# Three weight loads and the copies of shifted rows moved from SyncE's DMA queue to ScalarE's and GpSimd's

## The chip, the core and the metric

The kernel runs on one core of a Trainium2 chip. A core has five engines with an instruction stream each: TensorE (PE in the profile; its weight loads are PEld), VectorE (DVE), ScalarE (ACT), GpSimd (POOL) and SyncE (SP), which computes nothing and issues DMAs here. ACT and POOL can issue DMAs too. An engine works through its stream in order, and a wait for a semaphore holds back everything behind it in the same stream. The transfers themselves run on 16 DMA engines that all queues share.

The metric is the device time of one execution in microseconds (us); lower is better.

## What is computed

Two branches over one layer-normalised input, added to it. S = 2048 tokens, D = 448, 16 heads of 28, F = 1792, all inputs bf16.

```python
xn = layernorm(x)
# A: linear attention with learned feature maps
q, k, v = split_heads(xn @ wqkv)
phi = lambda t: concat(softmax(t @ w_phi), softmax(-(t @ w_phi)))
kv, z = phi(k)^T v, sum over tokens of phi(k)          # per head
attn = (phi(q) kv / (phi(q) z + 1e-6)) @ wo
# B: token shift and MLP, on xn again
h  = gelu(layernorm(xn) @ w1)
hs = concat(h[:, 0:112] one token later, h[:, 112:224] one earlier,
            h[:, 224:336] two later, h[:, 336:448] two earlier) @ w2
x1 = xn + hs
mlp = x1 + gelu(layernorm(x1) @ w3) @ w4
out = x + attn + mlp
```

## The kernel before

Everything stays in SBUF. Tokens are cut into 16 tiles of 128 (index `i`), features into chunks of up to 128. The kernel is first recorded: each call of `R.mm`, `R.act`, `R.ew`, `R.dma` and `R.dma_t` notes an instruction with the bytes it writes and reads, and `Recorder.solve` (L76) then derives the semaphore waits. So all instructions of a kind share a line in the profile (matmul L204, PE transpose L208, activation L212, elementwise on DVE or POOL L216, DMA transpose L219, DMA copy L222), and tiles are told apart by their names. The order of the calls is the order on each engine; it is written by hand, in three parts.

**The start (L366 to L388).** Loads are issued at once from SP and ACT: `xtok` (the tokens, in nine pieces), `wv`, `w1`, each weight in two halves, one per queue. SP goes on with the later tokens, `wphi`, and DMA transposes of `wqkv` columns into `wT`.

**The first phase, `chain([...])` (L949 to L969).** It normalises the tokens (`ln_stats` on DVE, `ln_scale` on POOL, `ln1_apply` on DVE or POOL; `ln1_sums(1)`, L470, gets the sums of tile 1 on ACT), transposes them into `xnT`, and runs the products with `wv` (`ZV`), with `w1` (`ZW` for the first 384 columns of h, `ZR` for the rest), and the folding of `w_phi` into the query and key weights (`FO`, whose result DVE casts into `wpq` and `wpk`). Pairs of matmuls on 64 rows each run on the two halves of the array; `chain` decides how the two halves interleave. Of its entries these matter here:

- `h_shift(gg)` (L669): h, transposed, lies in `hT` from column `OFF`; six DMA copies from SBUF to SBUF put rows 64 to 127 of each chunk, shifted by one or two tokens, into the front columns of `hT`. `gg` is the half of the tokens. `h_shift(0)` belongs to the entry `ZR(0, ...)` and is recorded when `chain` takes the last matmul of that entry's upper half; by then the next entry, `("p", 14)`, has been recorded, so POOL normalises tile 14 first. `h_shift(1)` stands near the end of the list.
- `rest_T(h)` (L666): a DMA transpose of the last 64 columns of h into `hRT`, on SP.
- `late_3` (L432): POOL clears the padding of `phik`, all of `kvq`, and part of `eq`. `kv_ones` (L438) then writes four blocks of ones into `kvq` on DVE.
- `kv_picks` (L731): POOL clears `pick`, DVE copies four blocks into it.
- `load_w2`, `load_w4` (L390, L395) and `load_lap(w3, B_w3)` (L358): weight loads, on SP, at the places where they stand in the list. `load_lap` takes the queues as its third argument.

**The second phase, `play([...])` (L1034 to L1054).** Here PE alternates between key and query products (`k0`, `k1`, `q0`, `q1`), the products of shifted h with `w2` (`w0`, `w1_`), kv tiles (`K`), the MLP with `w3` (`a`, `b`), attention numerators (`N`) and the final sums (`f`). Around the keys: ACT takes exponentials into `phik` (`k_exp`), DVE sums them (`kn`, L710), POOL multiplies by the reciprocal (`kx`, `k_product`, L717; eight products of two tiles each), and `K` i reads the result of `kx` i // 2. `sc`, `A` and `G` are the second layer norm: POOL's scale, the normalisation on POOL or DVE (`on_dve` lists tiles 4, 6, 7, 9, 12) into `g_tok`, and SP's DMA transpose into `gT`. The last `kx` is recorded as reading `g_tok`, so it waits for the normalisations of tiles 4 to 7. `wo_in` (L1030) loads `wo` between `kx` 5 and `kx` 6 of the list (counted from 0; the products 6 and 7 counted from 1).

Of the kernel before, what the change touches and what calls it, by code (L numbers as in the profile page):

```python
# [6 lines left out]
ACT = mybir.ActivationFunctionType  # L7
# [217 lines left out]
def bass_parallel_sum__linear_kernel_hedgehog__mixer_s_mlp__prompt_kernel(  # L225
    nc, A_x, A_wqkv, A_w_phi, A_wo, B_x, B_w1, B_w2, B_w3, B_w4, out,
):
    _, S, D = A_x.shape
# [6 lines left out]
    NH, REST = 3, 384  # L235
# [7 lines left out]
    with es:  # L243
        R = Recorder(nc, es)
# [9 lines left out]
        def view(h, cols, dt=BF16, at=0):  # L254
            a = h[:, at // 2:at // 2 + cols * DTB[dt] // 2]
            return a if dt == BF16 else a.bitcast(dt)

        def new(name, cols, dt=BF16):
            return view(region(name, cols * DTB[dt]), cols, dt)
# [13 lines left out]
        hT = view(hT_r, NH * HW).rearrange("p (m s) -> p m s", m=NH)  # L273
# [19 lines left out]
        w2 = new("w2", KC * D).rearrange("p (m d) -> p m d", m=KC)  # L293
        wo = wv
        w3 = new("w3", KC * F).rearrange("p (c f) -> p c f", c=KC)
        w4 = new("w4", FC * D).rearrange("p (c d) -> p c d", c=FC)
# [51 lines left out]
        dve, pool = "DVE", "POOL"  # L348


        def load_x(i, n, eng="SP"):
            R.dma(xtok[:, i:i + n, :], x2d[128 * i:128 * (i + n), :].rearrange("(j p) d -> p j d", p=128), eng)
# [5 lines left out]
        def load_lap(dst, src, engs=("SP", "SP")):  # L358
            for h in range(2):
                R.dma(dst[:, 2 * h:2 * h + 2, :], src[192 * h:192 * h + 256, :].rearrange("(c p) d -> p c d", p=128), engs[h])  # L360

        def load_half(dst, src, h, eng="SP"):
            R.dma(dst[:, 2 * h:2 * h + 2, :], src[192 * h:192 * h + 256, :].rearrange("(c p) d -> p c d", p=128), eng)
# [10 lines left out]
        load_x(5, 1, "ACT")  # L374
        load_half(w1, B_w1, 1)
        load_half(w1, B_w1, 0, "ACT")
        load_x(6, 2)
        load_x(8, 4)
        load_x(12, 4)
# [7 lines left out]
        load_wT(1, (0, 1, 2, 3))  # L387
        load_wT(0, (0,))  # L388

        def load_w2():  # L390
            R.dma(w2[:, 0:NH, :], B_w2[0:REST, :].rearrange("(m p) d -> p m d", p=128))
            for h in range(2):
                R.dma(w2[64 * h:64 * h + 64, NH, :], B_w2[REST:D, :])

        def load_w4():  # L395
            R.dma(w4[:, :, :], B_w4.rearrange("(c p) d -> p c d", p=128))

        vp = vaug.rearrange("p t (h e) -> p (t h) e", e=VP)

# [95 lines left out]
        def fold(t, m, b, n):  # L495
            def side(k, hi):
                r, c0, c1 = (slice(64, CR), 2 * DH, CR) if hi else (slice(0, 64), 0, 3 * DH)
                return [(banks[b + k][:, CR * c + c0:CR * c + c1],
                         wT[r, t, c, START[m + k]:START[m + k] + 128], bd[r, CR * c + c0:CR * c + c1], n == 0 and c == 0)
                        for c in range(NC)]  # L500
            return side(n, 0), side(1 - n, 1)
# [7 lines left out]
        def xn_T(i, b, n=1):  # L509
            return tuple([(xn_t(b)[:, h, 256 * j + 64 * kc:256 * j + 64 * kc + 64],  # L510
                           xn[lo:hi, i + j, 128 * kc:128 * kc + 128], ident[lo:hi, lo:hi], None)
                          for j in range(n) for kc in range(KC)] for h, (lo, hi) in enumerate((LO, HI)))
# [113 lines left out]
        def z_v(i, b):  # L626
            o = banks[b][:, 0:D]

            def make(rows, kcs):
                lo, hi = rows  # L630
                return [(o, xnT[lo:hi, kc, 128 * i:128 * i + 128], wv[lo:hi, kc, :], rows == LO and n == 0)
                        for n, kc in enumerate(kcs)]
            return make
# [11 lines left out]
        def z_w1(g, m, b):  # L645
            def make(rows, kcs):
                lo, hi = rows
                return [(banks[b], w1[lo:hi, kc, 128 * m:128 * m + 128], xnT[lo:hi, kc, 512 * g:512 * g + 512],
                         rows == LO and n == 0) for n, kc in enumerate(kcs)]
            return make  # L650
# [18 lines left out]
        def h_shift(gg):  # L669
            for m, r0, r1, q in ((0, 64, 112, 0), (1, 64, 96, 1), (2, 64, 80, 2), (0, 112, 128, 1), (1, 96, 128, 2),  # L670
                                 (2, 80, 128, 3)):
                s0 = max(0, 1024 * gg + SHIFTS[q])
                s1 = min(S, 1024 * gg + 1024 + SHIFTS[q])
                c0 = OFF + s0 - SHIFTS[q]
                R.dma(hT[r0:r1, m, s0:s1], hT[r0:r1, m, c0:c0 + s1 - s0])

        def w2_pair(i, b, heavy=None):
            def side(k, hi, rest):
# [223 lines left out]
        def do(f, *args):  # L902
            return "do", lambda: f(*args), ()

        def L(*ops):
            return do(ln1, *ops)

        def FO(t, m, n):
            return "both", fold(t, m, fb[t, m], n), ((fold_out, t, m, fb[t, m]),) if n else ()

        def XT(i, b, n=1, eng="ACT"):
            return "both", xn_T(i, b, n), ((xn_out, i, b, n, eng),)
# [4 lines left out]
        def ZV(i, *then):  # L917
            return "zip", z_v(i, vb[i]), then

        def ZW(g, m, *then):  # L920
            return "zip", z_w1(g, m, gb[g][m]), then

        def inside(n, job, inner):
            return (*job, (n, inner))

        def ZR(h, b, *then):
            return "zip", z_rest(h, b), then

        def EV(i, eng="ACT", n=1):
            return v_out, i, vb[i], eng, n  # L930

        def EW(g, m, n):
            return w1_out, g, m, gb[g][m], n
# [6 lines left out]
        def HF(p, n):  # L940
# [19 lines left out]
            ZW(1, 2, EW(1, 2, 1)), L(("p", 12), ("r", 15, 1)), inside(3, ZV(8, EV(8, "ACT", 1)), FO(1, 0, 0)), L(("m", 14)),  # L960
            XD(11), L(("r", 14, 1)), do(load_wT, 0, (1, 2, 3)), L(("a", 13)), inside(1, ZV(10, EV(10, "ACT", 1)), FO(1, 0, 1)),
            L(("a", 15)), ZR(0, 7, (rest_out, 0, 7), (rest_T, 0), (h_shift, 0)), ZV(9, EV(9, "DVE", 1)), XT(12, 3, 1, "ACT"),
            L(("p", 14)), do(load_w2), XT(13, 1, 1, "ACT"), ZV(11, EV(11, "ACT", 1)), ZW(2, 2, EW(2, 2, 1)), do(late_3),
            XT(14, 2, 2, "DVE"), ZW(2, 0, EW(2, 0, 1)), ZW(2, 1, EW(2, 1, 1)), do(load_lap, w3, B_w3), FO(1, 2, 0),
            inside(3, ZW(3, 0, EW(3, 0, 1)), FO(1, 2, 1)), ZR(1, 6, (rest_out, 1, 6)),
            inside(3, ZW(3, 2, EW(3, 2, 1)), FO(0, 0, 0)), ZV(15, EV(15, "ACT", 1)), do(kv_ones),
            inside(3, ZW(3, 1, EW(3, 1, 1)), FO(0, 0, 1)), do(rest_T, 1), inside(1, ZV(14, EV(14, "ACT", 1)), FO(0, 2, 0)),
            FO(0, 2, 1), ZV(13, EV(13, "ACT", 1)), ZV(12, EV(12, "DVE", 1)), HF(0, 0), do(kv_picks), HF(1, 0), HF(2, 0), HF(0, 1),
            do(h_shift, 1), HF(1, 1), do(load_w4), HF(2, 1)], 600, 1)  # L969

        on_dve = (4, 6, 7, 9, 12)
# [51 lines left out]
        def f(n, k):  # L1023
            fp[k][n - 1]()
# [3 lines left out]
            o_T(i)  # L1028

        def wo_in():  # L1030
            load_lap(wo, A_wo)

        K, G, S, T, kc, kb = kv_tile, g_T, store, q_T, kv_copy, kv_blocks
        play([  # L1034
# [4 lines left out]
            (w0, 8), (k1, 5), (q0, 5), (kx, 4), (K, 5), (lo, 4), (w1_, 8), (kn, 5), (q1, 5), (K, 6), (k0, 6), (w0, 10),  # L1039
            (k1, 6), (kx, 5), (q0, 6), (w1_, 10), (lo, 5), (q1, 6), (k0, 7), (K, 7), (kn, 6), (k1, 7), (q0, 7), (lo, 6),  # L1040
            (K, 8), (q1, 7), (lo, 7), (w0, 12), (kn, 7), (wo_in,), (kx, 6), (a, 0), (sc, 4), (w1_, 12), (b, 0), (A, 4),
            (G, 4), (A, 6), (K, 9), (A, 5), (G, 5), (G, 6), (a, 1), (K, 10), (A, 7), (K, 11), (b, 1), (a, 2), (K, 12),
            (b, 2), (kx, 7), (a, 3), (w0, 14), (a, 4), (G, 7), (lo, 9), (b, 3), (K, 13), (b, 4), (K, 14), (K, 15), (a, 5),
# [45 lines left out]
```

## Time and profile before

| What | Value |
|---|---|
| Time, median of 3 runs | 174.12 us (174.02 to 174.18) |
| The profiled execution | 174.06 us, span 172.3 us |
| PE busy / DVE / ACT / POOL | 97% / 64% / 48% / 52% of the span |
| DMA issues on SP / ACT / POOL | all but six / six / none |
| SP's issue of `w2` (3 DMAs), from 24.39 us | 2.56 us |
| SP's issue of `h_shift(0)`, from 28.31 us | 4.55 us |
| SP's issue of `w3` (2), from 32.90 us | 1.14 us |
| SP's issue of `h_shift(1)`, from 35.41 us | 3.85 us |
| SP's issue of `w4` (1), from 39.30 us | 0.59 us |
| SP's issue of `wo` (2), from 64.57 us | 1.09 us |

The span is the time from the first to the last instruction of the program in the profiled execution; the time of a run has 1.76 us around it. A timeline row gives its start and length in us, the engine, the line, the operation, what it writes and reads (`out<-in`) with shapes, how many instructions are merged (x3), and in brackets how long the engine sat idle before it and who ended that wait. SPq and ACTq are the parts of those engines that issue DMAs. Names have their numbers removed, so `w` stands for `w1`, `w2`, `w3` and `w4`, `vaug` also for buffers that later share its space. PE's busy time is modelled and its instructions overlap, so 97% doesn't mean that it is at its peak, but it does mean that there is next to no gap in which PE could catch up.

The chain of waits starts at the last instruction and goes back, at each step to what released the instruction or to the one before it on its engine. What is on it set the end.

### The profile page before, as it was taken

How to read it: one execution, taken by the hardware profiler on the slowest of the kernel's cores; microseconds unless marked ns; L12 is line 12 of the kernel's file. 1: busy time of each engine (PE TensorE's matmuls, PEld its weight loads, DVE VectorE, ACT ScalarE, POOL GpSimd, SP SyncE). 2: the span in 40 equal slices, each digit the busy share in tenths (PEclk: the TensorE clock that was granted, in tenths of full speed). 3: DMA queues.
4: the chain of work that ended last, by engine and by line, in shares of the span. 5: the costliest groups of instructions: out<-in, count | busy, mean ns of one | idle time of the engine just before them, and what ended most of it. 6: DMA issues, size and time to landing. Idle time of an engine off the chain costs nothing.

```text
span 172.3 us, 5315 instructions
## 1 busy us (share of the span) xinstructions
PE 166.9 (97%) x2308; PEld 96.6 (56%) x2308; DVE 110.9 (64%) x251; ACT 82.0 (48%) x107; POOL 90.0 (52%) x121
## 2 busy tenths in 40 slices
PE   7799999999999999999999999999999999999994
PEld 7545888874555555554544554554545545555563
DVE  3799943749999989918955873525817416474621
ACT  4478876777987899646133322133133212044000
POOL 5456970004779999860574289332441522724540
PEclk9999999999999999999999999999999999999999
DMA  5995546499998955161057557554961120233331
GB/s 127 330 248 92 104 67 158 87 352 220 334 159 174 135 124 138 21 76 30 11 114 97 111 105 146 94 103 106 136 135 34 30 57 4 57 34 84 88 87 50
DMA packets 51111, 20.07 MB, mean 116 GB/s; under 512 B 42256, under 2 KB 50384, under 8 KB 51088
## 3 DMA queue, kind: packets, MB, share of 16 engines
q1 hardware_dynamic: 49968, 18.86, 56.0%
q10 hardware_dynamic: 1120, 0.87, 1.6%
q8 instruction: 18, 0.29, 0.8%
q14 instruction: 5, 0.04, 0.1%
HBM read 7.14 MB, written 1.84 MB: 52 GB/s over the span
## 4 chain that ended last, share of the span: by engine, by line
PE 92%; DMA 3%; ACT 1%; DVE 1%; issue 0%; ACTq 0%
PE banks L204 91%; DMA wv<-in_A_wqkv_dram 3%; PE banks L208 1%; ACT xnT L212 1%; DVE wpq L216 1%; ACT vaug L212 0%; ACTq L222 0%; ACT L366 0%; DVE vaug L216 0%
## 5 line engine op out<-in xcount | busy, mean ns | idle before, releaser
L212 ACT ACTIVATE phik<-banks 128x1024 bf16<-128x1024 f32 (+1 forms) x44 | 42.2, 986 | 63.6 <-PE banks L204 63.4
L204 PE MATMUL banks<-gT,w 64*128 64x512 bf16 x392 | 49.2, 376 | 0.1
L216 DVE TENSOR_TENSOR vaug<-banks,vaug 128x464 f32<-128x464 f32 (+3 forms) x65 | 32.8, 513 | 20.6 <-PE banks L204 18.9
L204 PE MATMUL banks<-w,phik 64*128 64x448 bf16 (+3 forms) x434 | 45.2, 343 | 0.0
L216 POOL TENSOR_TENSOR xnT<-vaug 128x196 bf16<-128x196 f32 (+1 forms) x32 | 18.1, 587 | 47.8 <-DVE vaug L216 47.8
L204 PE MATMUL banks<-wv,xnT 64*128 64x448 bf16 (+3 forms) x222 | 32.8, 346 | 1.4 <-DMA wv<-in_A_wqkv_dram 1.2
L204 PEld LDWEIGHTS banks<-w,phik 64*128 64x128 bf16 (+1 forms) x434 | 22.9, 94 | 19.4 <-issue 0.4
L722 POOL TENSOR_TENSOR phik<-phik,rks 128x1792 bf16<-128x1792 bf16 x8 | 25.6, 3214 | 10.7 <-DVE rks L216 10.5
L204 PEld LDWEIGHTS banks<-gT,w 64*128 64x128 bf16 x392 | 18.0, 94 | 18.7 <-PE banks L204 1.1
L204 PEld LDWEIGHTS banks<-wv,xnT 64*128 64x128 bf16 (+1 forms) x222 | 13.8, 94 | 10.0 <-ACT xnT L212 1.6
L216 POOL TENSOR_TENSOR vaug<-xn,xtok 128x448 f32<-128x448 bf16 x16 | 16.2, 1033 | 0.2 <-DVE vaug L216 0.2
L216 DVE TENSOR_REDUCE ksum<-phik 128x64 f32<-128x1792 bf16 x8 | 16.0, 1994 | 0.0
L216 POOL TENSOR_TENSOR rs<-mv,mhalf 128x1 f32<-128x1 f32 (+2 forms) x18 | 12.4, 694 | 6.6 <-DVE mv L216 6.6
L204 PE MATMUL banks<-xnT,w 64*128 64x512 bf16 x84 | 15.7, 377 | 0.0
L216 DVE RECIPROCAL vaug<-banks 128x16 f32<-128x16 f32 x16 | 4.0, 252 | 17.4 <-PE banks L204 17.4
L204 PE MATMUL banks<-wpk,xnT 64*128 64x448 bf16 x112 | 14.9, 350 | 0.1
L212 ACT ACTIVATE hi<-banks 128x896 bf16<-128x896 f32 x16 | 13.8, 931 | 1.0 <-PE banks L204 1.0
L204 PE MATMUL banks<-wpq,xnT 64*128 64x448 bf16 x112 | 14.2, 349 | 0.0
L204 PE MATMUL banks<-w,hT 64*128 64x448 bf16 x96 | 12.9, 349 | 0.0
L216 DVE TENSOR_TENSOR xn<-banks,xn 128x512 bf16<-128x512 f32 (+1 forms) x16 | 9.0, 606 | 3.0 <-PE banks L204 2.9
L216 DVE BATCH_NORM_STATS2 st<-xn 128x6 f32<-128x448 bf16 x16 | 9.4, 589 | 0.0
L216 DVE BATCH_NORM_STATS2 st<-xtok 128x6 f32<-128x448 bf16 x15 | 9.1, 606 | 0.0
(72 smaller groups left out, 165.4 us busy)
## 6 DMA issues: line engine op xcount, KB each, us to landing
w<-in_B_w_dram SPq DMA_DIRECT2D x2, 896.0 KB, 5.7
out_dram<-vaug SPq DMA_DIRECT2D x15, 112.0 KB, 2.0
w<-in_B_w_dram SPq DMA_DIRECT2D x1, 1568.0 KB, 10.0
xtok<-in_A_x_dram SPq DMA_DIRECT2D x2, 448.0 KB, 7.4
wv<-in_A_wo_dram SPq DMA_DIRECT2D x2, 224.0 KB, 2.9
xtok<-in_A_x_dram SPq DMA_DIRECT2D x3, 112.0 KB, 2.6
xtok<-in_A_x_dram ACTq DMA_DIRECT2D x3, 112.0 KB, 2.8
w<-in_B_w_dram SPq DMA_DIRECT2D x1, 336.0 KB, 4.3
```

The costliest lines, as they stand in the source:

```text
L204: self.op("PE", lambda e: e.matmul(out, lhsT, rhs, start=start, stop=stop, skip_group_check=True), [out], [lhsT, rhs], tile=self._tile(lhsT))
L208: self.op("PE", lambda e: e.transpose(out, in_, ident), [out], [in_, ident], tile=self._tile(in_))
L212: self.op("ACT", lambda e: e.activation(out, in_, func, **kw), [out], [in_] + aps)
L216: self.op(eng, lambda e: getattr(e, name)(out, *args, **kw), [out], aps)
L722: R.op(pool, lambda e: e.tensor_tensor(ph, ph, wide, op=ALU.mult), [ph], [ph, wide, *after])
```

## The change

`w2` is issued by ACT right behind the ACT half of `w1`, at the very start, instead of by SP after the entry `("p", 14)`. The twelve copies of `h_shift` and the loads of `w3`, `w4` and `wo` keep their places in the order of calls, but POOL issues them instead of SP. ACT gets three more issues, POOL seventeen (six, two, six, one, two), SP loses twenty. What is transferred and computed stays the same; the waits that the copies need (for ACT's gelu, and of the second six for the first) go with them to POOL.

```diff
         load_half(w1, B_w1, 0, "ACT")
+        def load_w2():
+            R.dma(w2[:, 0:NH, :], B_w2[0:REST, :].rearrange("(m p) d -> p m d", p=128), "ACT")
+            for h in range(2):
+                R.dma(w2[64 * h:64 * h + 64, NH, :], B_w2[REST:D, :], "ACT")
+
+        load_w2()
         load_x(6, 2)
...
-        def load_w2():
-            R.dma(w2[:, 0:NH, :], B_w2[0:REST, :].rearrange("(m p) d -> p m d", p=128))
-            for h in range(2):
-                R.dma(w2[64 * h:64 * h + 64, NH, :], B_w2[REST:D, :])
-
         def load_w4():
-            R.dma(w4[:, :, :], B_w4.rearrange("(c p) d -> p c d", p=128))
+            R.dma(w4[:, :, :], B_w4.rearrange("(c p) d -> p c d", p=128), pool)
...
-                R.dma(hT[r0:r1, m, s0:s1], hT[r0:r1, m, c0:c0 + s1 - s0])
+                R.dma(hT[r0:r1, m, s0:s1], hT[r0:r1, m, c0:c0 + s1 - s0], pool)
...
-            L(("p", 14)), do(load_w2), XT(13, 1, 1, "ACT"), ZV(11, EV(11, "ACT", 1)), ZW(2, 2, EW(2, 2, 1)), do(late_3),
-            XT(14, 2, 2, "DVE"), ZW(2, 0, EW(2, 0, 1)), ZW(2, 1, EW(2, 1, 1)), do(load_lap, w3, B_w3), FO(1, 2, 0),
+            L(("p", 14)), XT(13, 1, 1, "ACT"), ZV(11, EV(11, "ACT", 1)), ZW(2, 2, EW(2, 2, 1)), do(late_3),
+            XT(14, 2, 2, "DVE"), ZW(2, 0, EW(2, 0, 1)), ZW(2, 1, EW(2, 1, 1)), do(load_lap, w3, B_w3, (pool, pool)), FO(1, 2, 0),
...
         def wo_in():
-            load_lap(wo, A_wo)
+            load_lap(wo, A_wo, (pool, pool))
```

On POOL the new issues stand in this order among its own work: the normalisation of tile 14, the six copies of `h_shift(0)`, the memsets of `late_3`, `w3`, the memset of `pick`, the six copies of `h_shift(1)`, `w4`, then the products of `kx` 0 to 5 (with the second layer norm of tiles 0 to 3 among them), `wo`, `kx` 6, the second layer norm of tiles 4 to 7, `kx` 7.

## The prediction

> **What bounds the kernel now.** I read the engine shares first, then the chain of waits in order of time, then the timelines of the engines whose queues the change touches.
>
> ```profile
> PE 166.9 (97%) x2308; PEld 96.6 (56%) x2308; DVE 110.9 (64%) x251; ACT 82.0 (48%) x107; POOL 90.0 (52%) x121
> PE banks L204 91%; DMA wv<-in_A_wqkv_dram 3%; PE banks L208 1%; ACT xnT L212 1%; DVE wpq L216 1%; ACT vaug L212 0%; ACTq L222 0%; ACT L366 0%; DVE vaug L216 0%
> ...
> 1.74 5.70 DMA wv<-in_A_wqkv_dram
> ...
> 30.18 1.10 DVE wpq L216
> ...
> 86.56 83.30 PE banks L204 x1012
> ```
>
> PE sets the end. The only transfer on the chain is the load of `wv`, which both kernels issue at the same place; after 31.3 us the chain is PE alone, but for four gaps of 0.05 us and the last 0.36 us. So nobody that matters waits for SP's queue, and emptying that queue earns nothing by itself. What can happen is that PE is made to wait. POOL is at 52% over the span, but a share of a span is an average; its timeline tells where it is full:
>
> ```profile
> 21.13 0.77 POOL L216 TENSOR_SCALAR xn<-xtok,rs 128x512 bf16<-128x512 bf16 x1
> 21.96 1.86 POOL L434 MEMSET phik<- 128x2048 bf16 x1
> 23.77 0.52 POOL L216 MEMSET kvq<- 128x512 bf16 x1
> ...
> 41.10 3.21 POOL L722 TENSOR_TENSOR phik<-phik,rks 128x1792 bf16<-128x1792 bf16 x1 [8.44 <-DVE rks L216]
> ...
> 60.37 9.55 POOL L722 TENSOR_TENSOR phik<-phik,rks 128x1792 bf16<-128x1792 bf16 x3
> 69.89 1.02 POOL L216 TENSOR_TENSOR rs<-mv,mhalf 128x4 f32<-128x4 f32 x1
> 71.00 0.20 POOL L216 TENSOR_SCALAR rs<-mv 128x4 f32<-128x4 f32 x1
> 71.42 1.03 POOL L216 TENSOR_SCALAR g_tok<-xn,rs 128x512 bf16<-128x512 bf16 x1 [0.22 <-POOL rs L216]
> 72.68 3.21 POOL L722 TENSOR_TENSOR phik<-phik,rks 128x1792 bf16<-128x1792 bf16 x1 [0.23 <-DVE g_tok L216]
> ```
>
> From 60.37 to 75.9 POOL works almost without a pause on the normalised keys, and PE follows it closely (PE's timeline):
>
> ```profile
> 75.31 0.39 PE L204 MATMUL banks<-vaug,phik 64*128 64x59 bf16 x16
> 75.55 0.81 PE L204 MATMUL banks<-gT,w 64*128 64x512 bf16 x6
> 76.19 0.62 PE L204 MATMUL banks<-vaug,phik 64*128 64x59 bf16 x32
> ```
>
> The last pair of kv tiles (76.19) reads the product that POOL ends at 72.68 + 3.21 = 75.89: 0.30 us of slack. At the start the engines that feed PE are as tight (timelines of ACT and DVE):
>
> ```profile
> 3.51 0.58 ACT L474 ACTIVATE xn<-xtok 128x448 bf16<-128x448 bf16 x1 [1.43 <-DMA xtok<-in_A_x_dram]
> ...
> 5.94 0.26 DVE L216 BATCH_NORM_AGGREGATE mv<-st 128x2 f32<-128x9 f32 x2
> 7.03 1.06 DVE L216 TENSOR_SCALAR xn<-xtok,mv,rs 128x512 bf16<-128x512 bf16 x3 [0.82 <-POOL rs L216]
> ...
> 27.93 0.46 DVE L216 MEMSET kvq<- 28x8 bf16 x4
> 30.18 2.18 DVE L216 CAST wpq<-banks 128x896 bf16<-128x896 f32 x2 [1.78 <-PE banks L204]
> ```
>
> **The change, part by part.** All against the profiled execution: span 172.3 us, 174.06 us with 1.76 us around it; the median of the runs is 174.12.
>
> *1. Three issues of `w2` on ACT, ahead of its first activation.* On SP the first two of these loads took 0.58 us each, all three 2.56 us with a full queue; ACT's own issues took 0.46 with 0.02 between. ACT's last issue now ends at 3.20, so the three end at 4.66 (0.46 each), 5.07 (0.6 each) or 5.80 (2.56 in all). The first activation starts there instead of 3.51; its statistics of token tile 1 took 1.70 us (3.51 to 5.21). They feed the second aggregate of the DVE row at 5.94, which begins near 6.02, 0.8 us later than needed. So the aggregate moves to 6.45, 6.85 or 7.6: late by 0.43, 0.8 or 1.5 us. Queued behind it on DVE: POOL's scale for tiles 1 and 2, DVE's normalisation (7.03), and PE's transposes of tile 2 at 7.58, which begin 0.18 us after it. DVE is then full to 20 us (1.93 of each 2.00 us), so I let the delay pass on whole. I take 0.8, the plain issue times of the same loads.
> The 448 KB are also moved earlier, into the 330 GB/s stretch of the token loads: 1.36 us for whoever shares the queues. The 448 KB load of tiles 8 to 11 landed 7.2 us after 3.68, at 10.9; at 12.3 it is still ahead of its statistics (11.68, now 12.5). Cost 0; without the 0.8 us before it, it would be 0.6.
>
> *2. The first six copies of hT rows, on POOL behind the row at 21.13.* Their inputs are done (ACT's last gelu of group 1 ends at 21.4), so they start at 21.96 instead of 28.31, and no wait is added. Each issue holds POOL for a time P that the trace doesn't show: POOL issues no DMA now. Bounds from the nearest rows, SP's issues of the same copies: 0.59 us (most of them) and 1.39 (the slowest); I take the middle, 0.99, say 1.0. Queued behind them on POOL: the memset of `kvq`, which ended at 24.29 and now ends at 24.29 + 6P. Behind it, on DVE, the four memsets at 27.93 (0.46 us), and behind those the cast of `wpq` at 30.18, which is on the chain. The cast starts at 24.84 + 6P: late by 6P - 5.34, that is 0 at 0.59, 0.66 at 1.0, 3.0 at 1.39. PE's fold waits in the same place, so all of it counts: 0.66.
> [...]
>
> *3. `w3`'s two loads and the second six copies.* At P = 1 POOL comes out of its memsets at 30.75, of `w3` at 32.8, of the memset for the picks at 33.2 (due 32.66; the DVE cast behind the picks has 0.7 us of idle time), of the copies at 39.2. PE wants them some 10 us later. Hidden by POOL's 8.44 us of idle time: cost 0.
>
> *4. `w4`.* 0.59 us on SP at least, at most until it landed (9.95 us); taken like the others, 1.0. POOL is then free at 40.2, ahead of its first product at 41.10 + 0.66. Cost 0; uncovered, the first kv tile still has 46.62 - 44.31 = 2.3 us, so it costs from an issue of 4.9 us on. SP loses w4's issue ahead of its transposes of q: they move earlier, with no reader before 80.69. Cost 0.
>
> *5. `wo`'s two loads, between POOL's products 6 and 7*, in the unbroken stretch that ends at 75.9. Product 7, the scale (69.89), DVE's three normalisations (71.23), POOL's own (71.42) and product 8 move by 2P. PE's tile at 71.30 waits first (product 7 ended at 69.92: slack 1.4), then the pair at 76.19 with 0.30. Cost 2P - 0.3: 0.9, 1.7 or 2.5. The transposes of g for group 1 move too; the last landed at 79.35 and is read at 81.08, which has moved as far. After 75.9 POOL rests for 7.7 us: nothing is carried on.
>
> *6. What leaves SP:* 2.56 + 4.55 + 1.14 + 3.85 + 0.59 + 1.09 = 13.8 us of issue. Copies and hRT land earlier; PE had no gap before reading them (33.6 to 36 us). Gain 0.
>
> Sum: 0.8 + 0.66 + 0 + 0 + 1.7 = 3.16; 174.06 + 3.16 = **177.2 us**. With all low ends: 0.43 + 0 + 0.9 = 1.3, 175.4. With all high ends: 1.5 + 3.0 + 2.5 = 7.0, 181.1.
>
> **The rivals.**
> *Cheap issue: not slower, 174.2 us.* POOL only hands a transfer over, as quickly as its smallest rows (memsets of 0.10 to 0.20 us). Then 2P is at most 0.4 against 0.3 of slack, 6P is far under 5.34, and what is left is the start, where PE's waits for ACT's copies (10.08 to 10.58, 12.39 to 12.99) could swallow the low end of 0.43. It decides from P below 0.2. For: SP's and ACT's issues are short and blind to size (0.39 to 0.59). Against: even those are two to three times too long.
> *POOL held by DVE: 179.7 us.* A row for it: POOL's normalisation at 71.42 took 1.03 us beside a DVE one of the same kind, 3.02/4 = 0.76 elsewhere. Beside the first six copies DVE runs a cast of 0.62, two copies of 0.75 together and a cast of 1.09: if each holds an issue for its length, 2.46 us more on the `kvq` memset, 177.2 + 2.5. Against: these DVE rows read PSUM. [...]
> *Issue that grows with the rows: 182.3 us.* `w4` has 1792 rows of 896 bytes, a hT copy at most 48. If POOL is held until `w4` has landed (9.95), it is free at 49.15, 7.4 us late; less 2.3 of slack that is 5.1 us of PE, on top of 3.16. Against: SP's issue of it was as short as the others.
>
> **How the numbers follow.** Forecast 0.62, cheap issue 0.13, POOL held by DVE 0.10, growing issue 0.15. The range 174.4 to 181.1 holds the forecast's own 175.4 to 181.1 and the second rival, and reaches down to the first; below and above lies about 0.2. A change under 0.2% (0.35 us) can't be told from none. Faster 0.05 and the same 0.08 share the cheap case (a gain beyond it has no row to come from); slower 0.87.
>
> **What would show it.** Right: POOL rows of hT copies near 1 us from 22 us on; the `kvq` memset ending near 30.3; DVE's `wpq` cast waiting for POOL; the first activation near 5; a PE gap of some 1.7 us in all at the kv tiles after 71 us. Wrong: POOL's DMA rows under 0.3 us or over 1.5; PE gaps elsewhere; or kv tiles that wait though POOL's products run on time.

## The result, and the profile after

The changed kernel takes 178.72 us (median of four runs: 177.81, 178.5, 178.95, 179.1), against 174.15 us of the kernel before in the same series: a ratio of 1.0248, 95% interval 1.0201 to 1.0295. The profiled execution took 178.5 us, with a span of 176.8 us, 4.5 us more than before. The ratios below leave out one execution, of run 11, which took 178.54 us at a clock of 0.98. The forecast of 177.2 us had the sign and nearly the sum, but none of its three terms had the size that was measured, and the largest single loss, by PE's clock, wasn't in it at all.

The page of the changed kernel, with the engine shares, the granted PE clock in 40 slices, and the shares of the chain by engine:

```profile
PE 169.6 (96%) x2308; PEld 97.6 (55%) x2308; DVE 111.1 (63%) x251; ACT 82.0 (46%) x107; POOL 100.0 (57%) x138
...
PEclk9858999999999999999999999999999999999999
...
PE 69%; POOL 15%; DVE 8%; ACT 3%; ACTq 2%; issue 1%; POOLq 0%
```

PE was 91% of the chain on one line alone; now POOL holds 15% of it and ACT's issues 2%. PE's busy time rose by 2.7 us though its work is the same: slices two to four show a clock below full. The chain of the changed kernel (start, length, what) shows both ends of this:

```profile
3.79 0.76 ACTq L222
4.58 0.65 ACTq L222
...
33.24 1.10 DVE wpq L216
...
69.84 0.75 POOL wv L222
70.60 0.72 POOL wv L222
...
77.41 3.22 POOL phik L723
80.68 3.80 PE banks L204 x64
...
91.06 83.30 PE banks L204 x1012
```

The `wpq` cast, at 30.18 before, is 3.06 us late. The last kv pair, at 76.19 before, starts 4.49 us late, so another 1.4 us is lost in between, with `wo`'s two issues (named `wv` here) and POOL's products ahead of it. From 91.06 on the chain is the same 83.30 us of PE that began at 86.56 before. So the loss is two pieces: 3.06 us by the `wpq` cast and 1.4 us at `wo`.

**The first piece.** Timelines of ACT, DVE and PE of the changed kernel:

```profile
2.77 2.46 ACTq L222 DMA_DIRECT2D w<-in_B_w_dram  x4
5.34 0.58 ACT L475 ACTIVATE xn<-xtok 128x448 bf16<-128x448 bf16 x1 [3.24 <-POOL rs L216]
7.07 0.20 DVE L216 BATCH_NORM_AGGREGATE mv<-st 128x2 f32<-128x9 f32 x1 [1.07 <-ACT xn L477]
7.57 0.48 PE L204 MATMUL banks<-wv,xnT 64*128 64x448 bf16 x1 [1.34 <-ACT xnT L212]
8.55 0.39 PE L208 MATMUL banks<-ident,xn 64*128 64x64 bf16 x8 [0.50 <-DVE xn L216]
31.00 0.46 DVE L216 MEMSET kvq<- 28x8 bf16 x4
```

ACT's first activation, at 3.51 before, comes after the three `w2` issues. DVE's aggregate of tile 1 is now a row of its own at 7.07, where it was due near 6.02: 1.05 us late. PE stands still for 1.34 us, up to 7.57, and for 0.50 more up to 8.55. Between the two, at 7.68, its clock halves, so the second gap can't have caused the fall. The windows of the changed kernel show it (window, its length, busy time of PE, PEld, DVE, ACT and POOL with instruction counts, then PE's clock, the DMA share and GB/s):

```profile
7.20:7.68 0.48, 0.11 (x1) 0.09 (x1) 0.06 (x1) 0.32 (x1) 0.34 (x1) 1.00 1.10 375
7.68:11.09 3.41, 2.91 (x26) 1.36 (x27) 2.94 (x9) 1.19 (x2) 1.82 (x4) 0.50 1.10 354
11.09:14.51 3.42, 3.42 (x27) 2.01 (x25) 3.28 (x11) 1.68 (x3) 1.63 (x4) 0.50 1.77 203
14.51:16.00 1.49, 1.49 (x21) 0.88 (x17) 1.46 (x5) 1.09 (x3) 0.97 (x2) 1.00 0.81 17
```

The clock is at half from 7.68 to 14.51 us. In the kernel before it was 1.00 throughout, with one gap of PE at this place, and PE wasn't full from 10 to 12 us (PE's timeline and a window of the kernel before):

```profile
7.57 0.35 PE L204 MATMUL banks<-wv,xnT 64*128 64x448 bf16 x1 [1.20 <-DMA wv<-in_A_wqkv_dram]
...
10.00:12.00 2.00, 1.83 (x20) 0.77 (x17) 1.93 (x6) 1.49 (x4) 1.12 (x3) 1.00 1.38 214
```

At half the clock PE is full from 11.09 us on. The queue's delay of 1.05 us leaves some 2.0 of the 3.06 to the clock; the experiments test this split.

**The second piece.** POOL's timeline of the changed kernel:

```profile
24.47 3.29 POOL L222 DMA_DIRECT2D hT<-hT  x6
29.50 0.54 POOL L216 MEMSET kvq<- 128x512 bf16 x1
...
38.77 1.12 POOL L222 DMA_DIRECT2D w<-in_B_w_dram  x1
...
69.80 1.52 POOL L222 DMA_DIRECT2D wv<-in_A_wo_dram  x2
...
77.41 3.21 POOL L723 TENSOR_TENSOR phik<-phik,rks 128x1792 bf16<-128x1792 bf16 x1 [0.55 <-DVE g_tok L216]
```

A hT copy holds POOL for 0.55 us on average, `w4` for 1.12, and a load of half `wo` for 0.76. The last product ends at 77.41 + 3.21 = 80.62, and PE's kv pair at 80.68 stood still for 1.00 us behind it. The copies, on the other hand, cost nothing on this path: `kvq` is cleared at 30.04, and DVE's ones at 31.00 don't wait for it.

### The profile page after: what moved, and what is told of

Same layout as the page of the kernel before. It is cut to its first block, busy times and chain, and to the rows that moved or that the text cites. A ratio compares the mean times of both kernels' runs of the same rounds, so it can differ in the third digit from the quotient of the medians.

```text
span 176.8 us, 5315 instructions
## 1 busy us (share of the span) xinstructions
PE 169.6 (96%) x2308; PEld 97.6 (55%) x2308; DVE 111.1 (63%) x251; ACT 82.0 (46%) x107; POOL 100.0 (57%) x138
## 4 chain that ended last, share of the span: by engine, by line
PE 69%; POOL 15%; DVE 8%; ACT 3%; ACTq 2%; issue 1%; POOLq 0%
PE banks L204 68%; POOL phik L723 11%; DVE ksum L216 3%; ACTq L222 2%; POOL rs L216 2%; POOL g_tok L216 2%; PE banks L208 2%; DVE xn L216 1%; ACT phik L212 1%; DVE rks L216 1%; POOL wv L222 1%; DVE g_tok L216 1%; DVE wpq L216 1%; DVE st L216 1%; ACT xn L477 0%
## 5 line engine op out<-in xcount | busy, mean ns | idle before, releaser
L204 PE MATMUL banks<-wv,xnT 64*128 64x448 bf16 (+3 forms) x222 | 35.4, 370 | 1.4 <-ACT xnT L212 1.3
L204 PEld LDWEIGHTS banks<-wv,xnT 64*128 64x128 bf16 (+1 forms) x222 | 14.6, 97 | 10.2 <-ACT xnT L212 2.9
```

The source lines that it names most:

```text
L204: self.op("PE", lambda e: e.matmul(out, lhsT, rhs, start=start, stop=stop, skip_group_check=True), [out], [lhsT, rhs], tile=self._tile(lhsT))
```

## The experiments

All ratios are against the kernel before in the same series (174.0, 174.25 or 174.21 us), with 95% intervals. They are worked out from all runs of a series and differ by up to 0.1% from the quotient of the two medians. The letters in the expectations stand for the theories as they were when the run was planned. "After" is the changed kernel.

| Run | What is moved | us | Ratio |
|---|---|---|---|
| 1 | `w2` at the start only | 177.09 | 1.0182 (1.0144 to 1.0220) |
| 2 | all but `w2` | 175.79 | 1.0106 (1.0084 to 1.0128) |
| 3 | all, more idle matmuls | 177.51 | 1.0204 (1.0173 to 1.0234) |
| 4 | `w2` only, more idle matmuls | 175.80 | 1.0103 (1.0068 to 1.0137) |
| 5 | all, `w2` later on ACT | 176.80 | 1.0139 (1.0062 to 1.0215) |
| 6 | `w2` later on ACT only | 174.32 | 1.0012 (0.9994 to 1.0030) |
| 7 | `wo` only | 176.10 | 1.0103 (1.0073 to 1.0133) |
| 8 | all, `w2` and `wo` later | 175.67 | 1.0081 (1.0045 to 1.0117) |
| 9 | all but `w2` and `wo` | 174.51 | 1.0037 (1.0013 to 1.0061) |
| 10 | copies only | 174.38 | 0.9999 (0.9981 to 1.0017) |
| 11 | run 9, eight more issues on POOL | 175.99 | 1.0089 (1.0062 to 1.0115) |
| 12 | run 3, copies back on SP | 179.35 | 1.0284 (1.0217 to 1.0350) |

### What `w2` costs, and how

*Run 1: `w2` alone.* The kernel before, with only this:

```diff
         load_half(w1, B_w1, 0, "ACT")
+        def load_w2():
+            R.dma(w2[:, 0:NH, :], B_w2[0:REST, :].rearrange("(m p) d -> p m d", p=128), "ACT")
+            for h in range(2):
+                R.dma(w2[64 * h:64 * h + 64, NH, :], B_w2[REST:D, :], "ACT")
+        load_w2()
...
-            L(("p", 14)), do(load_w2), XT(13, 1, 1, "ACT"),
+            L(("p", 14)), XT(13, 1, 1, "ACT"),
```

> Only w2 moves to ACT, all else as before. Theory (ACT's first activation waits behind the three issues, the second aggregate on DVE comes 1.05 us late, and PE's longer gap lets the granted clock fall to half for two stretches of 3.4 us): start 3.1 us later, about 177.2 us, first kv tile and last kv pair shifted by the same amount; 175.2 in an execution in which the clock holds. Rival A (POOL's copies and memsets are part of the start's loss): 174.5 to 175.5 even with the clock at half.

3.1 us lost. The first activation starts at 5.79, the aggregate at 7.52, 1.5 us late; PE stands for 1.71 and 0.62 us, and its clock is at half from 8.55 to 15.38; the `wpq` cast comes at 33.90, 3.72 us late in the profiled execution. The four runs differ by their mean clock: 177.72 and 177.54 us at 0.98, 176.63 and 176.49 at 0.99. So a part of the loss moves with the clock, about 1.1 us from 0.99 to 0.98. The last kv pair, at 79.91, is late by the same 3.72 us. Rival A is out: nothing on POOL was moved here, and as much is lost at the start.

*Run 2: all but `w2`.* The changed kernel, with `w2` on SP at its old place:

```diff
-                R.dma(w2[64 * h:64 * h + 64, NH, :], B_w2[REST:D, :], "ACT")
+                R.dma(w2[64 * h:64 * h + 64, NH, :], B_w2[REST:D, :])
...
-        load_w2()
...
-            L(("p", 14)), XT(13, 1, 1, "ACT"),
+            L(("p", 14)), do(load_w2), XT(13, 1, 1, "ACT"),
```

> The changed kernel with w2 back on SP at its old place; POOL still issues the copies, w3, w4 and wo. Theory: the start is as before (0), the last pair of kv tiles waits for POOL by two issues of wo less the slack, 1.54 - 0.30 = 1.2 us: 175.4 us, clock 1.0 throughout. Rival A (copies on POOL delay the cast of wpq, as the prediction had it): a DVE wait before the wpq cast, and about 176.

The clock is 1.0 in all four runs, and the `wpq` cast comes at 30.35, 0.17 us after its old time. All that is left is the second piece. PE's timeline of this kernel:

```profile
77.78 0.63 PE L204 MATMUL banks<-vaug,phik 64*128 64x59 bf16 x32 [1.00 <-POOL phik L722]
```

The kv pair starts 1.59 us later than before; less the 0.17 that is 1.42 us, as in the changed kernel.

*Run 3: hold the clock.* The start of the chain has five idle matmuls (`spin`), on data that nobody reads. The changed kernel, with fourteen:

```diff
-            XT(0, 2, 1, "ACT"), do(spin, 5, 256),
+            XT(0, 2, 1, "ACT"), do(spin, 14, 256),
```

> The changed kernel with 14 instead of 5 idle matmuls of 256 columns in PE's gap before the first product with wv (1 us more of PE work, in a gap of 1.3 us). Theory of the clock: the clock stays at 1.0, and of the start's 3.06 us about 2 come back: 176.7 us. Rival C (the start's loss is w2's 448 KB in the stretch of the token loads, or ACT's wait alone): no gain, 178.5 to 179.

The clock stays at 1.0. The `wpk` cast, which precedes that of `wpq`, in the kernel before, in the changed kernel and in this one (DVE's timelines):

```profile
20.67 1.09 DVE L216 CAST wpk<-banks 128x896 bf16<-128x896 f32 x1 [0.33 <-PE banks L204]
23.73 1.09 DVE L216 CAST wpk<-banks 128x896 bf16<-128x896 f32 x1 [0.77 <-PE banks L204]
21.66 1.09 DVE L216 CAST wpk<-banks 128x896 bf16<-128x896 f32 x1
```

It comes 2.07 us earlier than in the changed kernel and 0.99 later than before. That is the split: 2.07 us of clock and 0.99 of queue. But the loss against the kernel before fell by 1.1 us only (from 4.6 to 3.5), because the `wpq` cast came at 32.21. PE had stood for 0.63 us at 30.37 for the transposes of `wqkv`, whose last two landed at 28.68 and 30.32 us (24.71 and 25.96 before).

*Run 4: the same with `w2` alone.* Run 1 with `do(spin, 14, 256)`.

> w2 on ACT at the very start as the only part of the change (177.1 us in an earlier run), and 14 instead of 5 idle matmuls in PE's first gap. Theory of the clock: clock 1.0, what stays is the late first activation: wpk's first cast 1.0 to 1.4 us late instead of 3.1 to 3.7, 175.2 us. Rival (the clock's fall isn't what the time goes to): 177.

Run 1's loss of 3.1 us is now 1.6. The `wpk` cast moves from 24.39 to 21.67. A window of this kernel:

```profile
10.00:12.00 2.00, 1.83 (x25) 0.77 (x23) 1.93 (x7) 1.40 (x3) 1.24 (x2) 1.00 1.11 336
```

With the full clock PE again isn't the engine that is full here (1.83 of 2.00); DVE is (1.93). PE's gaps are 0.75 and 0.62 us. Two of the six runs show a clock of 0.99 and take 176.65 and 176.84 us, the other four, at 1.00, 175.25 to 176.11, at or above the 175.2 expected. So the idle matmuls only just suffice.

*Run 5: `w2` on ACT, but behind its copy of the first transposed tile.* The changed kernel with

```diff
-        load_w2()
...
-            XT(0, 2, 1, "ACT"), do(spin, 5, 256),
+            XT(0, 2, 1, "ACT"), do(load_w2), do(spin, 5, 256),
```

> The changed kernel with w2 still issued by ACT, but behind its copy of the first transposed tile, where ACT was idle for 1.72 us before. Theory (the start is lost in ACT's queue, ahead of the first activation, and then by the clock): first activation near 3.5, clock 1.0, only wo's cost is left: 175.6 us, as with w2 back on SP (175.8). Rival C (w2's 448 KB beside the token loads cost the time): still over 177.

Start and clock are as before (first activation 3.56, clock 1.0, `wpk` 20.51), yet the time is 1.2 us over the expectation. PE stands for 0.43 us at 23.02, for the transpose of a token tile, and for 0.49 us at 29.46, for the transposes of `wqkv`; the `wpq` cast comes at 31.30. The queue delay is gone, and late transposes have come in its place.

*Run 6: this move of `w2` alone, in the kernel before.*

```diff
-                R.dma(w2[64 * h:64 * h + 64, NH, :], B_w2[REST:D, :])
+                R.dma(w2[64 * h:64 * h + 64, NH, :], B_w2[REST:D, :], "ACT")
...
-            L(("p", 14)), do(load_w2), XT(13, 1, 1, "ACT"),
+            L(("p", 14)), XT(13, 1, 1, "ACT"),
...
-            XT(0, 2, 1, "ACT"), do(spin, 5, 256),
+            XT(0, 2, 1, "ACT"), do(load_w2), do(spin, 5, 256),
```

> The kernel before with one change: w2 issued by ACT behind its copy of the first transposed tile. It tells how much of the 1.0 us that the two kernels with this place of w2 lost at the cast of wpq belongs to w2's traffic beside the token loads, and how much to the copies on POOL. Theory E (both are needed: w2 pushes tokens and transposes back by about 1 us, which stays in their cover unless the copies share the DMA engines with the transposes): cast of wpq within 0.4 of 30.18, 174.1 to 174.5 us. Rival C (w2's traffic alone): cast near 31.3, 175.3 us.

No difference (a ratio of 1.0012), with `wpq` at 30.20. `w2` on ACT's queue, and its traffic beside the token loads, cost nothing here, where the issues stand behind ACT's first work.

### What `wo` costs

*Run 7: `wo` alone.* The kernel before with

```diff
-            load_lap(wo, A_wo)
+            load_lap(wo, A_wo, (pool, pool))
```

> The kernel before with one change: wo issued by POOL, between its products of the keys. Theory: two issues of 0.76 us less 0.30 us of slack at the last pair of kv tiles, a PE gap of about 1 us there and a little before it, 1.2 us: 175.3 us. Rival (POOL's late products are caught up elsewhere, or the loss in the changed kernel needs its other parts): 174.1.

1.9 us lost, 0.8 over the expectation. PE's waits in this kernel (who waits, for what: us in all, times, longest), in its profiled execution:

```profile
PE banks L204 <- POOL phik L722: 1.0, 1, 1.0
PE banks L204 <- DMA xnT<-xn: 0.4, 1, 0.4
```

The first is the loss foreseen: the kv pair starts at 78.11, 1.92 us late. The second, at 22.97, lies long before `wo`, where this kernel issues what the kernel before issues. A transpose landed at 22.93 instead of 20.71. It is 0.40 us of the 1.92 that isn't due to the edit, and leaves 1.5 for `wo`. It also shows that the transposes' landing differs between executions of the same code.

*Run 8: `wo` behind POOL's last product.* Run 5, and in the list of `play`:

```diff
-            (kn, 7), (wo_in,), (kx, 6),
+            (kn, 7), (kx, 6),
...
-            (b, 2), (kx, 7), (a, 3),
+            (b, 2), (kx, 7), (wo_in,), (a, 3),
```

> As the one before, and wo's two loads behind POOL's last product of the keys instead of ahead of the last but one; POOL then rests for 7 us. Theory: wo's 1.4 us go too, 174.3 us, like the kernel with w2 and wo back on SP (174.5); no PE gap at the last pair of kv tiles. Rival (wo's loads cost the same wherever POOL issues them, or arrive late for the final sums): no gain, or a PE gap behind 85 us.

PE's gap at the kv pair is gone. The median is 1.1 us below that of run 5, whose four runs spread over 1.6 us. It stays 1.4 us over the expectation and the kernel before: again late transposes, with PE gaps of 0.37 and 0.74 us, and `wpq` at 31.45.

### Copies, `w3` and `w4`

*Run 9: the changed kernel with `w2` and `wo` back on SP* (run 2, and `load_lap(wo, A_wo)`).

> The changed kernel with w2 and wo back on SP; POOL issues the twelve copies, w3 and w4. Theory: these cost nothing, 174.1 us (within 0.3 of before). Rival A: 0.7 us slower through the memset of kvq. Rival B (a less crowded SP queue is worth something): up to 0.5 us faster.

0.37% remains (0.13 to 0.61). The profiled execution is the slowest of the ten (176.11 us), and its timeline shows where such an execution loses:

```profile
36.06 0.36 PE L204 MATMUL banks<-w,hRT 64*128 64x448 bf16 x1 [1.63 <-DMA hRT<-gT]
```

The DMA view of this kernel, for the issues from 27.55 to 28.50 us (what, queue, kind and count, KB each, us to landing):

```profile
w<-in_B_w_dram POOLq DMA_DIRECT2D x2, 896.0 KB, 9.8
...
hRT<-gT SPq DMA_TRANSPOSE x1, 8.4
```

The same transpose in the kernel before (its DMA view):

```profile
hRT<-gT SPq DMA_TRANSPOSE x1, 2.5
```

There `w3` stood behind it and behind all six copies in SP's queue, 5.9 us later. Here POOL issues `w3` 0.07 us after it, and its two loads of 896 KB each are under way beside it, landing after 9.8 us (median; 5.7 in the kernel before). The transpose lands at 36.02, PE waits. It needn't come to that: in run 2's profiled execution POOL issued `w3` 0.74 us after this transpose, it landed within 3.3 us, and PE didn't wait. What the nine faster executions of run 9 lost isn't shown by any trace.

*Run 10: the twelve copies alone on POOL,* in the kernel before:

```diff
-                R.dma(hT[r0:r1, m, s0:s1], hT[r0:r1, m, c0:c0 + s1 - s0])
+                R.dma(hT[r0:r1, m, s0:s1], hT[r0:r1, m, c0:c0 + s1 - s0], pool)
```

> The kernel before with one change: the twelve copies issued by POOL; w2, w3, w4 and wo stay on SP. Theory E: the transposes of wqkv land 1 to 2 us later than before (24.7 and 26.0), most of it inside their cover: 174.1 to 174.6 us, cast of wpq within 0.4 of 30.18. Rival D alone (the copies cost the transposes' time in full): a PE wait for the transposes near 29 and 175 us.

No difference in time: the six issues take 0.49 to 0.76 us each, and `kvq` is cleared at 27.37, ahead of DVE's ones at 27.87. What theory E said of the transposes shows too: the last two of `wqkv` land at 26.00 and 28.68 us, 1.3 and 2.7 later than before, PE waits 0.27 us for them, and the cast of `wpq` comes at 30.57, 0.39 late.

*Run 11: is the path over `kvq` real?* Run 9, with eight small DMAs behind the first six copies, into a part of `w4` that its load overwrites later:

```diff
+            if gg == 0:
+                for n in range(8):
+                    R.dma(w4[0:16, n, 0:16], ident[0:16, 0:16], pool)
```

> The kernel with w2 and wo back on SP, and eight more DMAs on POOL behind the first six copies, of 16 rows of 32 bytes each into a part of w4 that its load overwrites later: issue time with next to no traffic. Theory (an issue holds POOL for 0.5 us whatever it moves; behind it the memset of kvq, the four memsets on DVE, the cast of wpq): kvq's memset 4 us later, near 31.3, the cast of wpq near 31.9 instead of 30.3, 1.6 us slower than its base (174.5): 176.1 us. Rival (the chain through kvq isn't there, or tiny issues cost nothing): 174.5.

The loss rises from 0.37% to 0.89%. POOL's and DVE's timelines of this kernel:

```profile
21.74 3.26 POOL L222 DMA_DIRECT2D hT<-hT  x6
25.00 3.84 POOL L222 DMA_DIRECT2D w<-ident  x8
...
30.57 0.54 POOL L216 MEMSET kvq<- 128x512 bf16 x1
...
31.20 0.46 DVE L216 MEMSET kvq<- 28x8 bf16 x4 [3.58 <-POOL kvq L216]
31.67 2.09 DVE L216 CAST wpq<-banks 128x896 bf16<-128x896 f32 x2
```

Eight issues of 0.48 us push the memset of `kvq` back until DVE waits for it, 3.58 us long, and the `wpq` cast with it, 1.49 us late. The path that step 2 described is there; the copies alone are too cheap to reach it.

*Run 12: run 3 with the copies back on SP,* to see whether it was the copies on POOL that made the transposes of `wqkv` late.

> The changed kernel with 14 idle matmuls in PE's first gap, and the twelve copies back on SP. With the copies on POOL that gap-filled kernel had the clock at 1.0 but still cast wpq 2.03 us late: 1.0 from the start, the rest behind a PE wait of 0.63 us for the transposes of wqkv. Theory D (the copies, now early on POOL's own queue, share the DMA engines with those transposes, which SP's single queue kept apart): the transposes land as before, no PE wait for them, the cast of wpq 1.05 us late, about 0.9 us faster than with the copies on POOL: 176.5 us. Rival (the transposes are late for another reason, the later start of SP's queue): the same wait, 177.5 us.

Both expected times were missed: its loss is 5.1 us where that of run 3 was 3.5. At the transposes theory D was partly right. The last two of `wqkv` land at 28.26 and 28.96, 0.42 and 1.36 us earlier than in run 3 though they were issued 0.41 later; PE no longer waits for them, and the `wpq` cast comes at 31.80 instead of 32.21. Against the kernel before they are still late, since SP issues them 2.7 and 1.8 us later. But a loss appears that neither theory had. PE's two new waits in this kernel:

```profile
PE banks L204 <- DMA hT<-hT: 0.5, 1, 0.5
PE banks L204 <- DMA hRT<-gT: 0.5, 1, 0.5
```

With no copies ahead of it, POOL issues `w3` at 26.30 and 27.24; the transpose into `hRT`, issued by SP at 26.15, takes 10.1 us, and the copies behind it land between 36.78 and 38.05 us. In the changed kernel the copies stand ahead of `w3` in POOL's own stream, and `w3` goes out at 30.43.

No version here is faster than the kernel before.

## Why the prediction came out as it did

*Step 1 failed in size: "I let the delay pass on whole. I take 0.8".* The path was right: issues, first activation, aggregate, normalisation, transposes of tile 2. The three issues took 0.49, 0.76 and 0.65 us instead of 0.6 each and ended at 5.23 instead of 5.07, the activation began 0.11 us behind them, and the aggregate moved by 1.05. That is the small error. The large one is that the sum held no term for PE's clock: the prediction says nothing of what PE's standing still does to it. The delay of 1.05 us became 3.06, since the clock fell to half for 6.83 us. Run 3 takes that part away by itself (2.07 us at the `wpk` cast) with the queue's delay left in place, and run 4 does so with `w2` as the only change. The 448 KB beside the token loads cost nothing, as said, at least where run 6 has them, from 5.96 us on.

*Step 2 had the mechanism right, and P wrong: "I take the middle, 0.99, say 1.0".* P measured 0.55, below the lower bound of 0.59 that SP's rows gave. Then 6P is 3.3, and the term 6P - 5.34 is nothing. In the changed kernel the ones at 31.00 follow the memset without a wait, run 10 shows no loss, and run 11 shows the path as soon as 14 issues stand there. An issue held POOL for 0.48 us (the small ones of run 11) up to 1.12 (`w4` in the changed kernel).

*Steps 3 and 4, cost 0: right for POOL's time in the changed kernel,* where `w4` took 1.12 us of the 4.9 it could have had. They left out the order of the transfers. Run 9, the changed kernel without `w2` and `wo`, still loses; in its profiled execution PE waits 1.63 us for the transpose into `hRT`, beside which `w3` passes, and in run 12 that transpose took 10.1 us beside `w3`.

*Step 5 right: "2P - 0.3", 1.7 us foreseen.* P is 0.76 for these, which would give 1.2; the measured 1.42 (changed kernel and run 2) and 1.5 (run 7) are 0.2 to 0.3 more. In the changed kernel product 8 starts 4.73 us late, 1.67 beyond the 3.06 of the first piece and so 0.15 more than the 1.52 that the two issues held POOL; PE starts 0.06 us behind its end. With the 0.30 of slack that is 1.67 - 0.30 + 0.06 = 1.43. Run 8 takes the loss away by issuing `wo` where POOL rests.

*Step 6, gain 0: right,* but of "copies and hRT land earlier" only the copies hold: with them on POOL, the first transpose into `hRT` landed at 31.32 in the changed kernel, 30.43 in run 2 and 36.02 in run 9, against 29.47 before.

*The sum.* 0.8 + 0.66 + 1.7 = 3.16 stood against 3.06 + 0 + 1.42 = 4.48 of the profiled execution's 4.5. That the forecast came within 1.5 us is partly luck: 2.26 us were missing at step 1, and 0.94 of it was made up by a P that was too large at steps 2 and 5.

*The rivals.* Cheap issue: P isn't under 0.2. POOL held by DVE: the six copies took 3.29 us in the changed kernel and 3.26 in run 11, 0.78 the first and some 0.50 each other, so there is no room for the 2.46 us that this rival added; in run 10 the two issues that ran beside DVE's cast from 24.06 to 24.68 took 0.51 us each, like the others. Issue that grows with the rows: it does, but only from 0.5 us (up to 48 rows) over 0.76 (256) to 1.12 (1792), far from the 9.95 us that it needed.

*The signs.* The first activation came at 5.34, near 5 as foreseen, and PE stood still for 1.00 us at the last kv pair, where 1.7 in all were named. The copies' rows were at 0.55 us and not near 1, and the `wpq` cast waited for PE and not for POOL: both speak against step 2. The `kvq` memset ended at 30.04, near the 30.3 foreseen, but by the later start of everything and not by P; had I looked at that sign alone, step 2 would have seemed right. PE's gaps at the start are the sign "PE gaps elsewhere", and they led to the missing term.

*What stays open* is the lateness of transposes in runs 3, 5 and 8 (1.4 us in run 8). In part the copies account for it. The last transpose of `wqkv` took 5.05 to 6.64 us in the seven runs in which POOL issued copies beside it (2, 3, 5 and 8 to 11; one profiled execution of each), 2.88 to 4.57 in those without (the kernel before, runs 1, 4, 6, 7 and 12), and 4.00 in the changed kernel, where the copies came only after it, from 24.47 on. Alone the copies cost no time that could be told from none (run 10), and `w2` at its later place cost none either (run 6). How much `w2` and `w3` add, and why a token transpose was late by itself (0.40 us in run 7, with nothing moved ahead of it), wasn't settled.

## What to carry to other kernels

Before work is put ahead of the first instruction of an engine that feeds PE, look at the granted clock around PE's next gaps: a delay of 1.05 us at the start cost 3.06 here, and 2.07 of them were the clock's, which 14 idle matmuls instead of 5 held up (run 3). Price a moved DMA issue by what its new engine does at that place, not by its share of the span: the same kind of issue was free in POOL's idle stretches and cost 1.4 us in its one full stretch. And a shared queue is also an order: a load that moves to its own queue passes beside the transfers that it used to stand behind, and they can take longer for it, as the transpose into `hRT` beside `w3` did (8.4 us in run 9, 2.5 in the kernel before).

## What the runs showed of the hardware

PE's clock went to half at 7.68 us in the changed kernel, after a gap of 1.34, and at 8.55 in run 1, after one of 1.71 and 0.16 of the next. It did not fall after one of 1.20 (before), nor after 0.75 and 0.62 with idle matmuls ahead (run 4's profiled execution). It stayed at half for 6.83 us both times. No gap ahead of either fall was over 1.71 us.

Of the 3.41 us (half of those 6.83) that ended with the fall PE was busy for 1.81 in the changed kernel and for 1.54 in run 1. Where the clock held, PE was busy for at least 2.20 (before), 2.11 (run 3) and 2.03 (run 4's profiled execution) of any 3.41 us after its first work. But the length of a gap doesn't settle it: in run 9 the clock held over one of 1.63 us, with 3.41 us of which PE was busy for only 1.78. What else decides isn't shown by any run. At half the clock PE was busy for 2.91 us (changed kernel) and 2.96 (run 1) of the first 3.41, and for all of the 3.42 behind them; then the clock was full again. The kernel before isn't safe from it: one of its 19 runs in the series of runs 5, 8, 11 and 12 shows a clock of 0.99 and took 176.03 us.

A DMA that POOL issues held it for about 0.5 us with 16 to 48 rows, 0.48 even for 16 rows of 32 bytes, 0.72 to 0.81 with 256 rows, of 896 bytes (`wo`) as of 3584 (`w3`), and 1.10 to 1.13 with 1792. The first DMA that POOL issued in an execution took 0.14 to 0.26 us more than its like later: 0.78 against 0.53 for a copy (changed kernel), 0.94 against 0.77 for `w3` (run 12) and against 0.80 for `wo` (run 7). ACT's first five issues took 0.40 to 0.49 us in the changed kernel, and the three of `w2` behind them 0.49 to 0.76; in run 12 one of these took 1.29.

The DMA transpose into `hRT` took 8.4 and 10.1 us where POOL issued `w3` within 0.15 us of it (runs 9 and 12), 3.3 where `w3` came 0.74 us later (run 2), and 2.5 in the kernel before, where `w3` came 5.9 us later on the same queue.
